# HGRN2 recurrence and multiplicative FFN: q, k and f of the first four chunks in their own buffers, issued ahead of the weights

## The chip, the cores and the metric

The kernel runs on one core of one Trainium2 chip. The metric is the device time in microseconds (us), as the median of several runs. The core has five engines with their own instruction queues: PE (TensorE, matrix products; PEld is its weight load), DVE (VectorE), ACT (ScalarE), POOL (GpSimd) and SP (SyncE). In this kernel SP issues every transfer between HBM and the on-chip memory. Each engine runs its queue strictly in the order in which the program emits it.

## What is computed

```python
def _attn_ref(q, k, v, f_logit):          # each (4, 8, 768, 48): batch, heads, steps, head size
    f = 1.0 / (1.0 + np.exp(-f_logit))
    for t in range(S):
        state = f[:, :, t, :, None] * state + np.einsum('bhd,bhe->bhde', k[:, :, t], v[:, :, t])
        y[:, :, t] = np.einsum('bhd,bhde->bhe', q[:, :, t], state)

def _moe_ref(x, w1, w2, w3, w_out):       # x (3072, 384), w1 w2 (384, 1024), w3 (1024, 1024), w_out (1024, 384)
    return ((x @ w1) * (x @ w2) @ w3) @ w_out
```

The outcome y of the recurrence, with heads side by side, is the x of the second part. The four weight matrices come as float64, so each is twice the bytes of its float32 form.

## The kernel before

**Tiling.** The 4 x 768 steps are cut into 24 chunks of 128 steps (`NU = 24`), six to a batch element. Four chunks make one FFN block of 512 rows (`NB = 6`). A chunk's work for all eight heads is laid out on 112 partitions (two groups of 48 with a gap of 16 rows) by 512 columns.

**One chunk `u`** (function `attention(u)`), with the keys of the tasks in brackets:

- loads of f, q and k (`lf`, `lq`, `lk`, L291, two DMAs of 96 KB each) and of v (`lv`, L300, one of 192 KB);
- ACT: gate = sigmoid(f) (`g`, L305). DVE: the forward product scan (`p`, L313), a reciprocal (`i`, L323), Q = q times the product (`q`, L329), the backward scan (`r`, L335), K = k times that (`k`, L343);
- PE: the K-Q pairs into PSUM (`a`, L352), ACT copies them (`m`, L361), POOL cuts them to the causal half (`c`, L367), PE multiplies by v and adds the state's share (`v`, L402 and L410 or L417);
- PE turns K (`t`, L378), ACT copies it (`e`, L386), PE forms the update of the state (`s`, L438), DVE applies it (`d`, L448 to L454), ACT lays it out for the next chunk (`b`, L460);
- ACT copies the outcome (`y`, L467). For the first four chunks PE moves it into the layout of x with the constant `perm` (`z`, L491) and ACT copies that (`x`, L496). For the others ten DMAs do it (L486).

**Buffers.** f and k have two buffers each, q three, v three, used in turn. So f of chunk 2 is loaded once the gate of chunk 0 has read its buffer, k of chunk 3 once K of chunk 1 has been formed, and so on. The gap rows 32 to 63 of every buffer are filled once by POOL in `setup()` (L235 to L237). `perm` occupies one of the four buffers of the pool "ab" until the first four chunks have been moved; POOL fills it by ten copies (L255).

**Weights.** w1 and w2 come as three pieces of 1 MB each (L879), w_out as four of 768 KB, w3 as eight of 1 MB (by the profile's list of issues). They land in five raw buffers; from the sixth piece on, a piece takes a raw buffer whose former content has been converted. Converting 512 columns to float32 takes two ACT instructions (L897, L900) and four on DVE (L903, L904, L908, L914). The FFN's first products need the first half of all three w1 pieces, the second ones that of all three w2 pieces. Later PE multiplies w3 by w_out once (L964, eight groups), so that the down product uses that single matrix; from the second block on, a scheme with seven products in place of eight is used, for which DVE forms sums.

**Order.** All tasks are entered into a planner with an engine, a cost in us, their dependencies and a priority. `Plan.order()` repeatedly takes the task that can start first by these costs, and among equals the one with the lowest priority number; the resulting order is then emitted. Transfers are two tasks: the issue on SP and the time on one modelled "DMA" engine, one after another. So a dependency in the plan only sets the place in a queue; what an instruction waits for on the chip is the data and the buffers themselves.

```python
        t["lf"] = moves(0.87, 197, 250, load(fs[u % 2], f_logit), past(u, 2, "g"), n0 - 30)
        t["lq"] = moves(0.87, 197, 250, load(qs[u % 3], q), past(u, 3, "q"), n0 - 29)
        t["lk"] = moves(0.87, 197, 250, load(ks[u % 2], k), past(u, 2, "k"), n0 - 28)
```

Here `n0` is 0, 1, 2, 3 for the first four chunks and 45 and up for the others; v has n0 - 27, the pieces of w1 have -26 to -25.8, those of w2 -16.5 to -16.3.

Of the kernel before, what the change touches and what calls it, by code (L numbers as in the profile page):

```python
# [36 lines left out]
F32 = mybir.dt.float32  # L37
# [3 lines left out]
ALU = mybir.AluOpType  # L41
AF = mybir.ActivationFunctionType
# [3 lines left out]
P = 128  # L46
# [4 lines left out]
R = 64 + D  # L51
DM = H * D
# [3 lines left out]
TB = 512  # L56
# [3 lines left out]
NQ = HP * C  # L60
# [5 lines left out]
KH = KF // 2  # L66
# [107 lines left out]
def ranged(ctx, tc, q, k, f_logit, v, w1, w2, w3, w_out, out, ident, w12, wc, left):  # L174

    nc = tc.nc
# [7 lines left out]
    abp = ctx.enter_context(tc.tile_pool(name="abp", bufs=4))  # L184
# [7 lines left out]
    gate = [keep.tile([R, NQ + 1], F32, name=f"gate{i}") for i in range(2)]  # L192
# [11 lines left out]
    def at(a, *shape):  # L204
        n = 1
        for m in shape:
            n *= m
        t = place[:, a : a + n]
        return t.rearrange("p (a b) -> p a b", a=shape[0]) if len(shape) == 2 else t
# [4 lines left out]
    wos = at(10240, KF, DM)  # L214
# [2 lines left out]
    wct = [at(6144 + KH * DH * i, KH, DH) for i in range(4)]  # L217
    ups = {(nm, i): at(a + 2 * TH * i, TH) for nm, a in (("u2", 9216), ("u3", 9216 + TH)) for i in range(2)}
    abs_ = [at(10240 + KH * P * i, KH, P) for i in range(4)]
    dns = {nm: at(12288 + DH * i, DH) for i, nm in enumerate(("m1", "u2", "u3"))}  # L220

    plan = Plan()
    plan.slot("f", NF)
    plan.slot("a", 2)
    plan.slot("ab", 4)
    moving = plan.add("PE", 0.0, lambda: None, takes=["ab"], prio=-1e9)

    def heads(t):
        return t.rearrange("p (h c) -> p h c", c=C)

    def setup():
        nc.scalar.activation(warm, nc.const_aps.tensor(0.0, (R, 1), F32), AF.Sigmoid)
        for i in range(3):
            if i < 2:
                nc.gpsimd.memset(fs[i][32:64], 30.0)  # L235
                nc.gpsimd.memset(ks[i][32:64], 0.0)
            nc.gpsimd.memset(qs[i][32:64], 0.0)  # L237
            if i == 0:
                make_identity(nc, ident)
        nc.vector.memset(floor, FLOOR)  # L240
        nc.vector.memset(heads(floor)[:, :, 0], 1.0)
        nc.vector.memset(back, 0.0)
        for t in gate:
            nc.vector.memset(t[:, NQ : NQ + 1], 0.0)
        nc.vector.memset(ones, 1.0)
        for t in sb:
            nc.vector.memset(t, 0.0)

        nc.gpsimd.memset(perm, 0.0)
        for i, (kc, hp) in enumerate(met):  # L250
            for par in range(2):
                for r, t, at_, n in runs(2 * hp + par):
                    if t == kc:
                        a = 64 * par + at_
                        nc.gpsimd.tensor_copy(perm[:, i, r : r + n], ident[0:R, a : a + n])  # L255
# [19 lines left out]
    def past(u, n, *names):  # L275
        return [tk[u - n][nm] for nm in names if u >= n and nm in tk[u - n]]

    def moves(issue, size, rate, emit, deps, prio):

        i = plan.add("SP", issue, emit, deps, prio, lag=0.6)  # L280
        return plan.add("DMA", size / rate, lambda: None, [i], prio, lag=1.3)

    def attention(u):
        s, t = st[u], tk[u]
        opens, closes = u % NCH == 0, u % NCH == NCH - 1
        n0 = need(u)

        def load(dst, src):
            def emit():
                for par in range(2):  # L290
                    nc.sync.dma_start(dst[rows(par)], src[u, par])  # L291
            return emit

        t["lf"] = moves(0.87, 197, 250, load(fs[u % 2], f_logit), past(u, 2, "g"), n0 - 30)
        t["lq"] = moves(0.87, 197, 250, load(qs[u % 3], q), past(u, 3, "q"), n0 - 29)
        t["lk"] = moves(0.87, 197, 250, load(ks[u % 2], k), past(u, 2, "k"), n0 - 28)

        def load_v():
            s["v"] = loads.tile([P, DM], F32, name="vt")
# [2 lines left out]
        t["lv"] = moves(0.45, 197, 320, load_v, past(u, 3, "v", "s"), n0 - 27)  # L302

        def gates():
            nc.scalar.activation(gate[u % 2][:, 0:NQ], fs[u % 2][0:R], AF.Sigmoid)  # L305

        t["g"] = plan.add("ACT", 0.65, gates, [t["lf"]] + past(u, 2, "r") + past(u, 3, "d"), n0)
        if not opens:
# [17 lines left out]

        def scale_q():
            s["Q"] = work3.tile([R, NQ], F32, name="Q")
            nc.vector.tensor_tensor(s["Q"], qs[u % 3][0:R], s["P"], ALU.mult)  # L329

        t["q"] = plan.add("DVE", 0.7, scale_q, [t["p"], t["lq"]] + past(u, 3, "v", "a"), n0 + 0.1)

# [7 lines left out]

        def scale_k():
            s["K"] = work.tile([R, NQ], F32, name="K")
            nc.vector.tensor_tensor(s["K"], ks[u % 2][0:R], s["R"], ALU.mult)  # L343

        t["k"] = plan.add("DVE", 0.7, scale_k, [t["r"], t["lk"]] + past(u, 2, "a", "t"), n0)

        def pairs():
            s["pa"] = ps.tile([P, 2, NQ], F32, name="pa")
# [498 lines left out]
            q["m4"]["frees"].append(first_ab[1])  # L847


    pieces, folds, users = {}, [], []  # L850
    parts, w12_sums, wc_sums, joins, spot = [], [], [], {}, [0]

    def fetch(loads_, a, prio, subs, deps=()):

        total = subs[-1][1]
        if not wide:  # L860
            def plain():
                for place_, src in loads_:
                    for c0, c1, dst, _, _ in subs:
                        d = dst().rearrange("p (a m) -> p a m", a=a)
                        m = (c1 - c0) // a
                        b0 = c0 // a if len(subs) > 1 else 0
                        nc.sync.dma_start(d[place_], src[:, :, b0 : b0 + m])
            waits = [d for sub in subs for d in sub[4]]
            ld = plan.add("SP", 1.9 * total / 512, plain, waits, prio, lag=2.0)
            return [ld] * len(subs)  # L870
        load_no = len(users)
        buf = load_no if load_no < len(raws) else (load_no - len(raws)) % NRAW
        raw = raws[buf][:, 0 : 2 * total]
        words = raw.rearrange("p (n two) -> p n two", two=2)
        held = [g for no, b_, gs in users if b_ == buf for g in gs]

        def load():
            for place_, src in loads_:
                nc.sync.dma_start(raw.rearrange("p (a m) -> p a m", a=a)[place_], src.bitcast(U32))  # L879

        ld = moves(0.45, total, 380, load, held[-2:], prio)
        got = []
        users.append((load_no, buf, got))
        ends = []

        def sub(c0, c1, dst, due, waits):
            n = c1 - c0
            w = n / 512
            lo, hi = words[:, c0:c1, 0], words[:, c0:c1, 1]
            a0 = spot[0] if n <= 512 else (spot[0] + 512) // 1024 * 1024 % 2048  # L890
            spot[0] = (a0 + (512 if n <= 512 else 1024)) % 2048
            m = magnitudes[:, a0 : a0 + n]
            mine = range(a0 // 512, (a0 + n + 511) // 512)
            s = {}

            def magnitude():
                nc.scalar.activation(m, hi.bitcast(F32), AF.Abs)  # L897

            def rest():
                nc.scalar.activation(lo.bitcast(F32), lo, AF.Copy, bias=2.0, scale=2.0**-51)  # L900

            def shifted():
                nc.vector.tensor_scalar(m, m, HIGH, LOW, ALU.min, ALU.max)  # L903
                nc.vector.tensor_scalar(m.bitcast(U32), m.bitcast(U32), 3, None, ALU.logical_shift_left)  # L904

            def signed():
                s["to"] = dst()
                nc.vector.scalar_tensor_tensor(  # L908
                    s["to"].bitcast(U32), hi, 0x80000000, lo, ALU.bitwise_and, ALU.bitwise_or
                )  # L910

            def joined():
                to = s["to"].bitcast(I32)
                nc.vector.tensor_tensor(to, m.bitcast(I32), to, ALU.add)  # L914

            past = [joins[i] for i in mine if i in joins]
            b = plan.add("ACT", 0.2 + 0.43 * w, magnitude, [ld] + past, due)
            e = plan.add("ACT", 0.2 + 0.43 * w, rest, [ld], due)
            h = plan.add("DVE", 0.32 + 0.54 * w, shifted, [b], due)
            g = plan.add("DVE", 0.16 + 0.53 * w, signed, [e, b] + list(waits), due)  # L920
            j = plan.add("DVE", 0.16 + 0.53 * w, joined, [h, g], due - 1)
            parts.append((g, j))
            joins.update({i: j for i in mine})
            got.append(g)
            ends.append(j)

        for one_ in subs:
            sub(*one_)
        return ends

    def weights():
# [16 lines left out]
        def held(buf):  # L948
            return [g for _, b, gs in users if b == buf for g in gs]

        done = []
        for i in range(0, KF, 2):
            src = w_out[i * P : (i + 2) * P].rearrange("(kc p) c -> p kc c", p=P)
            done += fetch([(slice(0, P), src)], 2, 25 + 2.2 * i, [(
                0, 2 * DM, lambda i=i: wos[:, i : i + 2].rearrange("p a c -> p (a c)"), 45 + 2.2 * i, held(4),
            )])

        w3s = {}
# [71 lines left out]
        nc.vector.tensor_scalar(left, count, R - 0.5, None, ALU.is_lt)  # L1030

    setup()
    weights()
    for u in range(NU):
        attention(u)
        if u == NU - 1:
            judged = plan.add("DVE", 1.5, judge, [tk[i]["y"] for i in range(NU)], -20)
        if u % UB == UB - 1:
            ffn(u // UB)
# [340 lines left out]
```

## Time and profile before

| | |
|---|---|
| median of 4 runs | 509.95 us (508.39 to 511.66) |
| the profiled execution: its own time | 512.46 us |
| its span, first to last instruction | 510.6 us |
| PE busy | 489.1 us (96%) |
| DVE busy | 362.3 us (71%) |
| ACT busy | 162.3 us (32%) |
| POOL busy | 41.1 us (8%) |
| first matmul starts | 8.42 us |
| first FFN product starts (L512) | 41.88 us |
| mean granted PE clock | 0.993 |

The share of busy time is an average over stages. The page's second part cuts the span into 40 slices of 12.8 us with a digit for each engine: 9 is 90% busy or more. The chain of waits follows the work that ended last backwards through what released it. In its lines the first number is the start in us, the second the length; "SPq" is SP issuing a transfer, "DMA k" the time until that transfer landed.

### The profile page before, as it was taken

The numbers are of one execution on the slowest core, as the hardware profiler recorded it, in microseconds if no ns is written. First come the engines' busy times: TensorE is split into PE (matmuls) and PEld (weight loads), VectorE is DVE, ScalarE is ACT, GpSimd is POOL, SyncE is SP. The second block draws the span as 40 slices with busy tenths as digits, with TensorE's granted clock in tenths as the row PEclk, the third lists the DMA queues.
The fourth block names the chain that finished last, engine by engine and source line by source line (L and its number), as shares of the span: only waits on it lengthen the run. The fifth ranks groups of instructions, "written<-read, shape, count | busy, mean of one in ns | idle before, by whom it ended". The sixth has DMA issues, their size and how long they took to land.

```text
span 510.6 us, 8802 instructions
## 1 busy us (share of the span) xinstructions
PE 489.1 (96%) x3346; PEld 409.4 (80%) x3346; DVE 362.3 (71%) x701; ACT 162.3 (32%) x340; POOL 41.1 (8%) x48
## 2 busy tenths in 40 slices
PE   3879999999999999999999999999999999999995
PEld 2769754666689877889888889888899888889994
DVE  6869899999998749965678666255564677665541
ACT  3759545754334426311342112321010011011000
POOL 7120010110102111000210000010000000000000
PEclk9979999999999999999999999999999999999999
DMA  5986455854222356311251001210002100000011
GB/s 166 376 234 203 142 190 215 284 186 120 77 62 76 86 147 197 98 38 28 59 168 44 1 3 31 59 51 0 2 21 58 48 1 0 1 0 1 31 50 50
DMA packets 30163, 46.02 MB, mean 90 GB/s; under 512 B 6560, under 2 KB 20384, under 8 KB 28320
## 3 DMA queue, kind: packets, MB, share of 16 engines
q1 hardware_dynamic: 30112, 45.38, 28.8%
q8 instruction: 28, 0.46, 0.4%
q14 instruction: 23, 0.19, 0.1%
HBM read 36.70 MB, written 4.72 MB: 81 GB/s over the span
## 4 chain that ended last, share of the span: by engine, by line
PE 89%; DMA 5%; DVE 2%; SPq 1%; issue 1%; POOL 0%; ACT 0%; DVEq 0%; POOLq 0%; ACTq 0%
PE f L512 66%; PE f L964 8%; PE pa L352 4%; PE pa L402 4%; DMA k<-in_k_dram 2%; DMA vt<-in_v_dram 2%; PE pk L438 2%; PE pa L417 2%; PE pk L378 2%; DMA q<-in_q_dram 1%; SPq L291 1%; PE f L410 1%; PE f L402 1%; PE f L491 1%; DMA f<-in_f_logit_dram 0%
## 5 line engine op out<-in xcount | busy, mean ns | idle before, releaser
L512 PE MATMUL f<-xt,w 128*128 128x256 f32 (+1 forms) x600 | 159.6, 397 | 0.0
L512 PEld LDWEIGHTS f<-xt,w 128*128 128x128 f32 x600 | 113.0, 190 | 24.5 <-issue 10.0
L512 PE MATMUL f<-place 128*128 128x192 f32 (+1 forms) x504 | 114.1, 351 | 0.0
L512 PEld LDWEIGHTS f<-place 128*128 128x128 f32 x504 | 87.3, 190 | 6.9 <-issue 1.1
L367 POOL TENSOR_SCALAR_AFFINE_SELECT A<-A 128x1024 f32<-128x1024 f32 x24 | 31.6, 1316 | 299.8 <-ACT A L361 299.8
L964 PE MATMUL f<-place 128*128 128x384 f32 x128 | 43.1, 490 | 0.0
L615 ACT COPY a<-f 128x256 f32<-128x256 f32 x36 | 13.4, 372 | 78.0 <-PE f L512 59.5
L512 PE MATMUL f<-xt,place 128*128 128x256 f32 x144 | 37.1, 380 | 0.0
L964 PEld LDWEIGHTS f<-place 128*128 128x128 f32 x128 | 23.8, 190 | 15.8 <-issue 0.5
L512 PE MATMUL f<-wc,ab 128*128 128x192 f32 x192 | 35.6, 329 | 0.0
L352 PEld LDWEIGHTS pa<-Q,K 48*128 48x128 f32 x384 | 25.8, 204 | 10.4 <-issue 8.1
L352 PE MATMUL pa<-Q,K 48*128 48x128 f32 x384 | 30.5, 303 | 3.3 <-DVE K L343 3.3
L512 PEld LDWEIGHTS f<-wc,ab 128*128 128x128 f32 x192 | 31.8, 190 | 0.9
L313 DVE TENSOR_TENSOR_SCAN fwd<-gate,floor 112x512 f32<-112x512 f32 x24 | 30.2, 1257 | 2.7 <-ACT gate L305 1.9
L361 ACT COPY A<-pa 128x1024 f32<-128x1024 f32 x24 | 24.2, 1010 | 24.0 <-PE pa L352 24.0
L639 DVE TENSOR_TENSOR place<-f,a 128x256 f32<-128x256 f32 x36 | 15.3, 424 | 23.3 <-PE f L512 23.2
L335 DVE TENSOR_TENSOR_SCAN bwd<-gate,back 112x512 f32<-112x512 f32 x24 | 29.7, 1238 | 0.8
L512 PEld LDWEIGHTS f<-xt,place 128*128 128x128 f32 x144 | 26.9, 189 | 3.6 <-DVE place L639 0.2
L343 DVE TENSOR_TENSOR K<-k,bwd 112x512 f32<-112x512 f32 x24 | 17.6, 733 | 9.3 <-DMA k<-in_k_dram 5.9
L897 ACT ACTIVATE place<-place 128x512 f32<-128x512 f32 (+2 forms) x24 | 21.2, 885 | 8.7 <-DVE w L914 4.5
L467 ACT ACTIVATE ys<-pa 112x512 f32<-112x512 f32 x20 | 11.9, 596 | 36.4 <-PE pa L417 21.1
L900 ACT ACTIVATE place<-place 128x512 f32<-128x512 uint32 (+2 forms) x24 | 21.1, 892 | 7.4 <-DMA place<-in_w_out_dram 4.2
(97 smaller groups left out, 620.5 us busy)
## 6 DMA issues: line engine op xcount, KB each, us to landing
place<-in_w_dram SPq DMA_DIRECT2D x14, 1024.0 KB, 5.4
f<-in_f_logit_dram SPq DMA_DIRECT2D x48, 96.0 KB, 2.7
q<-in_q_dram SPq DMA_DIRECT2D x48, 96.0 KB, 2.7
k<-in_k_dram SPq DMA_DIRECT2D x48, 96.0 KB, 2.5
vt<-in_v_dram SPq DMA_DIRECT2D x24, 192.0 KB, 3.1
out_dram<-o SPq DMA_DIRECT2D x24, 192.0 KB, 2.0
place<-in_w_out_dram SPq DMA_DIRECT2D x4, 768.0 KB, 5.3
xt<-ys SPq DMA_DIRECT2D x120, 24.0 KB, 1.8
```

What stands on the lines that cost most here:

```text
L313: nc.vector.tensor_tensor_scan(s["P"], gate[u % 2][:, 0:NQ], floor, 0.0, ALU.mult, ALU.max)
L335: nc.vector.tensor_tensor_scan(s["R"][:, ::-1], gate[u % 2][:, NQ:0:-1], back[:, ::-1], 0.0, ALU.mult, ALU.max)
L343: nc.vector.tensor_tensor(s["K"], ks[u % 2][0:R], s["R"], ALU.mult)
L352: nc.tensor.matmul(s["pa"][:, par, cols], lhsT=s["K"][rows(par), cols], rhs=s["Q"][rows(par), cols], start=True, stop=True,)
L361: nc.scalar.copy(s["A"].rearrange("p r h c -> p r (h c)"), s["pa"])
L367: nc.gpsimd.affine_select(out=a, in_=a, pattern=[[0, H], [1, C]], compare_op=ALU.is_ge, fill=0.0, base=0, channel_multiplier=-1,)
L402: nc.tensor.matmul(y_block(b)[64 * half : 64 * half + w], lhsT=s["v"][:, h * D : h * D + w], rhs=s["A"][:, par, hp], start=bank not in met ...
L512: nc.tensor.matmul(out_, lhsT=lhs[i], rhs=rhs[i], start=start and i == 0, stop=i == len(lhs) - 1, skip_group_check=True,)
L639: nc.vector.tensor_tensor(ups["u3", k], q["Y"], q["a"], ALU.add)
L897: nc.scalar.activation(m, hi.bitcast(F32), AF.Abs)
L900: nc.scalar.activation(lo.bitcast(F32), lo, AF.Copy, bias=2.0, scale=2.0**-51)
L964: nc.tensor.matmul(w3s["p", jc], lhsT=w3s[jc][:, kc * P : kc * P + P], rhs=wos[:, kc], start=(kc == 0), stop=(kc == KF - 1),)
```

## The change

- k of chunks 2 and 3 and f of chunks 2 and 3 get a place of their own: one more of the four "ab" buffers, called `early`, held until K of chunks 2 and 3 has been formed (the task `coming`). q of chunk 3 gets a place inside the tile `place`, which w_out takes later; the conversion of w_out waits for Q of chunk 3.
- For the first four chunks the loads of f, k and q have no dependency. Their priorities are n0 - 30, n0 - 29.5 and n0 - 29, in that order (before: f, q, k with -30, -29, -28). All weight tasks are entered after the fourth chunk's.
- From chunk 4 on the buffers go round as before (f and k two, q three), and the plan lets these loads start only after the fifth weight piece (`asked[4]`, the second of w2) has landed.
- `setup()` fills the gap rows of the new places: two memsets of 32 x 1024 and one of 32 x 512 more on POOL, ahead of `perm`.

```diff
+    early = abp.tile([P, KH, TB], F32, name="ab")[0:R]
+    ks += [early[:, 0], early[:, 1]]
+    fs += [early[:, 2], early[:, 3]]
+    qs.append(at(12288, NQ)[0:R])
...
+    coming = plan.add("PE", 0.0, lambda: None, takes=["ab"], prio=-1e9)
...
+        nc.gpsimd.memset(early[32:64, 2:4], 30.0)
+        nc.gpsimd.memset(early[32:64, 0:2], 0.0)
+        nc.gpsimd.memset(qs[2][32:64], 0.0)
+        nc.gpsimd.memset(qs[3][32:64], 0.0)
...
-        t["lf"] = moves(0.87, 197, 250, load(fs[u % 2], f_logit), past(u, 2, "g"), n0 - 30)
-        t["lq"] = moves(0.87, 197, 250, load(qs[u % 3], q), past(u, 3, "q"), n0 - 29)
-        t["lk"] = moves(0.87, 197, 250, load(ks[u % 2], k), past(u, 2, "k"), n0 - 28)
+        fu, qu, ku = (x[u if u < 4 else u % n] for x, n in ((fs, 2), (qs, 3), (ks, 2)))
+
+        def free(n, *names):
+
+            if u < 4:
+                return []
+            return asked[4:5] + [tk[u - n if u - n >= 4 else u % n][nm] for nm in names]
+
+        t["lf"] = moves(0.87, 197, 250, load(fu, f_logit), free(2, "g"), n0 - 30)
+        t["lk"] = moves(0.87, 197, 250, load(ku, k), free(2, "k"), n0 - 29.5)
+        t["lq"] = moves(0.87, 197, 250, load(qu, q), free(3, "q"), n0 - 29)
...
+        if u in (2, 3):
+            t["k"]["frees"].append(coming)
...
         ld = moves(0.45, total, 380, load, held[-2:], prio)
+        asked.append(ld)
...
-                0, 2 * DM, lambda i=i: wos[:, i : i + 2].rearrange("p a c -> p (a c)"), 45 + 2.2 * i, held(4),
+                0, 2 * DM, lambda i=i: wos[:, i : i + 2].rearrange("p a c -> p (a c)"), 45 + 2.2 * i,
+                held(4) + [tk[3]["q"]],
...
     setup()
-    weights()
     for u in range(NU):
         attention(u)
+        if u == 3:
+            weights()
```

More of the change, by code (lines that the diff above doesn't have):

```diff
@@ L232, in setup @@
         nc.scalar.activation(warm, nc.const_aps.tensor(0.0, (R, 1), F32), AF.Sigmoid)
[L233 to L236, printed above, removed]
+        for i in range(2):
+            nc.gpsimd.memset(fs[i][32:64], 30.0)
+            nc.gpsimd.memset(ks[i][32:64], 0.0)
             nc.gpsimd.memset(qs[i][32:64], 0.0)
@@ L304, in gates @@
         def gates():
-            nc.scalar.activation(gate[u % 2][:, 0:NQ], fs[u % 2][0:R], AF.Sigmoid)
+            nc.scalar.activation(gate[u % 2][:, 0:NQ], fu, AF.Sigmoid)
         t["g"] = plan.add("ACT", 0.65, gates, [t["lf"]] + past(u, 2, "r") + past(u, 3, "d"), n0)
@@ L328, in scale_q @@
             s["Q"] = work3.tile([R, NQ], F32, name="Q")
-            nc.vector.tensor_tensor(s["Q"], qs[u % 3][0:R], s["P"], ALU.mult)
+            nc.vector.tensor_tensor(s["Q"], qu, s["P"], ALU.mult)
         t["q"] = plan.add("DVE", 0.7, scale_q, [t["p"], t["lq"]] + past(u, 3, "v", "a"), n0 + 0.1)
@@ L342, in scale_k @@
             s["K"] = work.tile([R, NQ], F32, name="K")
-            nc.vector.tensor_tensor(s["K"], ks[u % 2][0:R], s["R"], ALU.mult)
+            nc.vector.tensor_tensor(s["K"], ku, s["R"], ALU.mult)
         t["k"] = plan.add("DVE", 0.7, scale_k, [t["r"], t["lk"]] + past(u, 2, "a", "t"), n0)
+        if u in (2, 3):
+            t["k"]["frees"].append(coming)
         def pairs():
@@ L847, in ffn @@
             q["m4"]["frees"].append(first_ab[1])
-    pieces, folds, users = {}, [], []
+    pieces, folds, users, asked = {}, [], [], []
     parts, w12_sums, wc_sums, joins, spot = [], [], [], {}, [0]
```

## The prediction

> **What bounds the kernel now.** I read the page's slices first, for where PE is not busy.
>
> ```profile
> PE   3879999999999999999999999999999999999995
> DVE  6869899999998749965678666255564677665541
> PEclk9979999999999999999999999999999999999999
> ```
>
> PE is full from the fourth slice (38 us) to the last. The open part is the first 38 us: PE starts at 8.42 us, and the third slice is at 7 in both busy share and clock. The busy table by stretch gives that hole its size (the columns PE, PEld, DVE, ACT, POOL are busy us, then clock, DMA share, GB/s):
>
> ```profile
> 24.00:26.95 2.95, 2.95 (x42) 2.53 (x40) 2.74 (x5) 2.95 (x7) 0.71 (x1) 1.00 1.05 361
> 26.95:30.23 3.28, 0.01 (x1) 0.03 (x1) 0.83 (x2) 0.76 (x2) 0.77 (x1) 0.82 0.99 321
> 30.23:36.10 5.87, 5.87 (x42) 5.31 (x43) 5.70 (x12) 2.28 (x4) 1.36 (x1) 0.52 0.71 177
> 42.04:87.24 45.20, 45.20 (x212) 30.15 (x212) 42.51 (x74) 27.78 (x48) 1.42 (x1) 1.00 0.57 183
> 87.24:141.40 54.16, 54.16 (x335) 33.69 (x335) 52.77 (x68) 29.18 (x46) 5.16 (x4) 1.00 0.54 174
> 141.40:384.00 242.60, 241.36 (x1895) 209.65 (x1894) 166.71 (x344) 69.50 (x165) 19.85 (x15) 1.00 0.22 62
> ```
>
> PE stands still for 3.28 us and then runs 5.87 us at clock 0.52. From 42 to 384 us it is idle for 1.24 us in all. DVE is 94% and 97% busy from 42 to 141 us. The chain of waits names the cause of the hole:
>
> ```profile
> 10.83 7.14 DMA vt<-in_v_dram
> 17.98 0.02 issue
> 17.99 0.33 SPq L879
> ...
> 18.42 0.37 SPq L291
> 18.79 0.04 issue
> 18.84 10.46 DMA k<-in_k_dram
> ...
> 29.39 0.70 DVE K L343
> 30.10 0.14 issue
> 30.23 2.08 PE pa L352 x16
> 32.31 1.90 PE f L402 x15
> 34.21 1.90 PE f L410 x8
> 36.11 0.38 PE pk L378 x4
> 36.49 1.02 PE f L402 x15
> ```
>
> k of chunk 3 is issued at 18.42 us, behind three or four 1 MB weight pieces, and lands at 29.3, 10.46 us later (k's median over the run is 2.5 us). It was issued that late for two reasons. It needs the buffer of k of chunk 1. And SP has at most eight DMAs under way: the weight piece at 17.99 starts the moment v of chunk 1 has landed, which is the eighth DMA before it. The last lines show the clock's price: the same 15 matmuls of L402 take 1.90 us cold and 1.02 us warm.
>
> **The change, part by part.**
>
> *Issue order on SP.* A 96 KB load costs SP 0.44 us (0.87 for two), a v load 0.42. By the priorities the first 26 DMAs are 24 q, k and f loads with v of chunks 0 and 1 among them, then w1's three pieces, v of chunk 2, two w2 pieces. Before, 19 DMAs took from 1.35 to 10.36 us, 0.47 each; so w1 starts at 1.35 + 26 x 0.47 = 13.6 instead of 10.36. The other two w1 pieces went out at 13.54 and 13.97 before and go at about 14.0 and 14.5 now. All f, k, q of the first four chunks are out by 13.5 and down by 16, k of chunk 3 at about 13 instead of 29.3. The limit of eight does not bite: eight issues take 3.5 us, landing takes 2.3 to 2.8.
>
> A rule speaks against this order: the Trainium skill, "DMA: Bandwidth & Descriptors", section "Bandwidth", says to batch transfers to 1 MiB or more for three quarters of peak. The row behind it here: in the first 8 us of the run DMA share was 0.49 at 142 GB/s, with small loads only, against 0.99 to 1.05 later. By the rule the weights should lead: 3.2 us of half-used engines is lost to w1. By the trace that is covered. ACT first waited for w1 until 17.37 us (1.5 us), and DVE's first conversion ran only at 25.29. With w1's first piece landing at 13.6 + 4.4 (the shortest landing of a piece) = 18.0 and each next one about 3.5 us later (f of chunk 4, held by the eight, was let go by the second piece at 21.6, v of chunk 3 by the third at 24.9: 3.4 apart), all w1 is in by 25. Without that cover the price is the 3.2 us. I take 0.
>
> *POOL.* The memset of 32 x 512 takes 0.52 us; the two of 32 x 1024 are bounded by twice that, so 2.6 us more ahead of the ten copies that ended at 10.41, now 13.0. Behind them is the first causal cut, which started at 12.54 (its input at 12.47): 0.4 us later. Its product at 15.23 waits on PE behind L378, which waits for DVE's K; so 0. SP waits for these memsets too: that of f for chunk 2 ends by about 5.4, its load is issued at 6.9. 0.
>
> *v of chunk 0* moves from 6.17 to about 8.9 and lands at 11.3 to 12.1 (2.4 to 3.2 us). L438 used it at 11.34. So 0 to 0.7 us on chunk 1, since DVE's S stands ahead of K there; I take 0.4. v of chunk 3 waits for chunk 0's last use (17.2) and lies behind two w2 pieces, at about 31; before, it was first used 4.2 warm us of PE after K of chunk 3. So the covering work just ends there.
>
> *DVE.* Two waits for k go: 1.22 us (chunk 2) and 2.62 us (chunk 3), and 1.5 us of conversion that stood before the second are done after it. The first may come back: S of chunk 1 stands behind K of chunk 2 and waits for PE until 19.7. So K of chunk 3 starts at 29.39 - 2.62 - 1.48 + 0.4 = 25.7, or 24.5 if the 1.22 is kept.
>
> *PE.* At 25.7 + 0.8 = 26.5 its pairs are ready; PE's earlier work ended at 26.95 (plus up to 0.4). So the gap closes. From 30.23 to 42.04 PE was busy without a break, 11.81 us; L352, L402 and L410 cold took 2.08 + 1.90 + 1.90 against 1.09 + 1.02 + 1.06 warm, 2.7 us more. Warm it is 9.1, and FFN starts at 27.2 + 9.1 = 36.3 instead of 42.04: 5.7 us earlier. Its first weights: three conversions at 2.15 us and the state's 0.9 us after K give 25.7 + 0.7 + 7.4 + 0.8 (a stretched one, as L904's 1.20 us) = 34.6. In time.
>
> The clock is where a rule and the trace differ. Here a gap of 3.28 us cost 5.87 us at half clock, 2.7 us. The skill's page "TensorE: Matmul & The Clock Gate" gives one idle window of about 3.4 us for going cold and as much busy time for getting warm: by that no loss, or 1.7 us. The trace decides: 2.7. If a gap of 1 to 2 us stays, the page says warm; the trace shows no such gap, so its price lies between 0 and 2.7. I take 0, since the gap closes.
>
> *Downstream.* The gain has to pass the stage in which DVE is 94 to 97% busy. DVE itself is ahead by 29.39 - 25.7 = 3.7 (its 1.5 us of moved work included: 2.2), plus the 1.54 us it waited for ACT at 37.98 (ACT waited for the cold L410): 3.7 net. The slacks add: conversion of the last w2 piece ended about 1.2 us before PE needed it at 54.81, that of the last w_out piece at 84.91 for the fold at 87.24, 2.3 us. So PE can keep 3.7 + 1.2 = 4.9 of its 5.7. Loads from chunk 4 on are asked for after w2; they were first used at 43.99. 0.
>
> Sum: 0 (start) - 5.7 (hole and clock) + 0.8 (DVE) = -4.9. Against the profiled execution (span 510.6, its own time 512.46) that is a span of 505.7 and a time of 507.6. The median of the runs, 509.95, gives 505.0.
>
> **The rivals.**
>
> *The gain stays in the start.* Chunk 1 a full 0.7 us late, the S wait back, a gap that keeps the clock cold for 2.7 us, w1 landing late: 5.7 - 0.3 - 2.7 - 1 = 1.7, so 508.3. For it: ACT waits in order for w1, DVE is the fuller engine after 42 us. Against: PE has 9 us of queued work there.
>
> *SP's queue blocks the late weights (slower).* SP is in order. k of chunk 6 was issued at 68.05, when K of chunk 4 had been formed, and v at 76.95 after chunk 4's products; the last w_out piece went at 62.2, ahead of both. The plan is drawn anew, and if it puts that piece behind such a v, it goes 14.7 us later; less the slack of 2.3 and the 4.9 won, 7.5 us are lost: 517.4. Behind the k alone (5.9 us) nothing is lost on balance. It decides from about 10 us of delay. Against: the plan's costs put it right before, and chunk 4's work keeps its late priority.
>
> *It doesn't do what it says:* k of chunk 3 still late, by the limit of eight or by a memset. The issue times above exclude both; 510.
>
> *More:* the 1.22 us and all of DVE's stalls kept: 6.5 us, 503.5.
>
> **The numbers.** -4.9 (503.9 to 507): 0.50. More than 6: 0.09. Stays in the start: 0.17, of which a third is still faster by over 0.5% (2.55 us, about what a measurement of this kernel can tell from no change). SP blocks or another re-drawn queue: 0.22, nearly all slower. Nothing: 0.02. So faster 0.63, same 0.15, slower 0.22. The range runs from 502.5 to 514: it leaves out half of the slower cases and a little below.
>
> **What would show it.** K of chunk 3 on DVE before 26.5 us without a DMA wait; no PE gap over 1 us after 20 us and clock 1.00 from there; first L512 at 35.5 to 37.5; first w1 piece down at 17.5 to 18.5; first fold (L964) at 82 to 83.5; no new idle time on PE after that. It is wrong if L512 starts on time but the fold does not, if ACT or DVE waits for w1 by more than 3 us, or if SP waits for a K or a product with w_out or w3 behind it.

## The result, and the profile after

| | before | after |
|---|---|---|
| median, all runs | 509.93 us (63 runs, 507.43 to 514.33) | 508.46 us (42 runs, 506.56 to 511.26) |
| ratio after / before | | 0.9969, 95% interval 0.9959 to 0.9980 |
| the profiled execution's own time | 512.46 us | 506.82 us |
| its span | 510.6 us | 504.5 us |
| first FFN product, first fold (w3 by w_out; L964, now L984), on PE's timeline | 41.88, 87.24 us | 36.28, 83.10 us |

The change makes the kernel 0.31% faster, about 1.5 us, where 4.9 us were forecast. The two profiled executions differ by 5.6 us in their own times. So the profiles seem to say that the forecast came true, and the medians say that two thirds of it did not. Both profiles are out of the ordinary: the one before lies 2.5 us above its kernel's median, the one after 1.6 us below, the second shortest of the 44 executions of the changed kernel that have a recorded clock. Most of what follows is about that contradiction.

The page's slices after the change (tenths busy, 12.6 us each; line numbers after the change are 8 to 20 higher than before):

```profile
PE   3899999999999999999999999999999999999995
PEclk9999999999999999999999999999999999999999
```

The 7 of the third slice is gone from PE and from the clock. The busy table by stretch, with the columns as before:

```profile
24.00:26.95 2.95, 2.79 (x34) 2.48 (x32) 2.88 (x5) 2.95 (x6) 1.02 (x1) 1.00 1.02 429
26.95:30.23 3.28, 3.28 (x52) 2.77 (x50) 3.21 (x5) 3.17 (x7) 1.67 (x2) 1.00 0.86 351
30.23:36.10 5.87, 4.67 (x56) 3.99 (x56) 5.66 (x14) 3.99 (x10) 0.04 (x1) 1.00 0.68 203
36.28:83.10 46.82, 46.82 (x227) 31.68 (x225) 45.04 (x78) 29.92 (x54) 1.42 (x1) 1.00 0.59 190
```

The stretch 26.95 to 30.23, in which PE stood still before, is full; the next runs at clock 1.00, with 1.2 us of new waiting in it. After 36.28 us nothing new is lost: the last row has PE busy throughout, so has the stretch from there to 135.5, and in the 244.5 us after that PE is idle for 0.70. The span is 6.1 us shorter, though the fold starts only 4.1 us earlier. The other 2.0 us lie behind the fold; half of them are waits of PE for K (0.7 us) and for v (0.3) that the profile before has there and this one has not. The chain of waits shows what holds the start now:

```profile
13.45 6.91 DMA place<-in_w_dram
20.39 1.59 DVE Q L345
...
25.41 0.68 DVE Q L345
...
32.25 0.43 DVE place L923
33.08 0.61 PE pk L396 x4
...
36.35 1.49 PE f L530 x6
```

k is no longer in it. From 20.4 to 32.7 us the chain runs through DVE: Q and K of the chunks, then three weight conversions. PE's own timeline has the new wait (start, length, what ran, and in brackets the idle time before it and its cause):

```profile
26.44 1.16 PE L370 MATMUL pa<-Q,K 48*128 48x128 f32 x16
...
33.08 0.61 PE L396 MATMUL pk<-ident,K 112*128 112x112 f32 x4 [1.01 <-DVE S L471]
...
36.28 1.56 PE L530 MATMUL f<-xt,w 128*128 128x256 f32 x6
...
39.03 2.32 PE L530 MATMUL f<-xt,w 128*128 128x256 f32 x10
```

The pairs of chunk 3 (L370) start at 26.44 without a wait. PE then waits 1.01 us for S, the state after chunk 2 (L471), which stands behind those conversions on DVE.

### The profile page after: what moved, and what is told of

Its sections match the earlier page's. It is cut to its first block, busy times and chain, and to the rows that moved or that the text cites. A ratio compares the mean times of both kernels' runs of the same rounds, so it can differ in the third digit from the quotient of the medians.

```text
span 504.5 us, 8806 instructions
## 1 busy us (share of the span) xinstructions
PE 486.2 (96%) x3346; PEld 407.2 (81%) x3346; DVE 362.4 (72%) x701; ACT 162.6 (32%) x340; POOL 42.5 (8%) x51
## 4 chain that ended last, share of the span: by engine, by line
PE 92%; DVE 2%; DMA 1%; POOL 1%; SPq 1%; issue 1%; POOLq 0%; DVEq 0%
PE f L530 69%; PE f L984 8%; PE pa L370 4%; PE pa L420 4%; PE pa L435 2%; PE pk L456 2%; PE pk L396 2%; DMA place<-in_w_dram 1%; SPq L299 1%; DVE Q L345 0%; DVE w L933 0%; DVE w L927 0%; PE f L509 0%; DVE bwd L351 0%; DVE fwd L329 0%
## 5 line engine op out<-in xcount | busy, mean ns | idle before, releaser
L984 PE MATMUL f<-place 128*128 128x384 f32 x128 | 43.1, 490 | 0.0
L984 PEld LDWEIGHTS f<-place 128*128 128x128 f32 x128 | 23.8, 190 | 15.8 <-issue 0.5
L370 PEld LDWEIGHTS pa<-Q,K 48*128 48x128 f32 x384 | 24.8, 198 | 6.9 <-issue 4.2
L370 PE MATMUL pa<-Q,K 48*128 48x128 f32 x384 | 29.5, 296 | 0.0
L485 ACT ACTIVATE ys<-pa 112x512 f32<-112x512 f32 x20 | 11.9, 598 | 40.6 <-PE pa L435 23.0
L396 PE MATMUL pk<-ident,K 112*128 112x112 f32 x80 | 12.3, 280 | 11.2 <-DVE K L359 10.2
```

What stands on the lines that cost most here:

```text
L370: nc.tensor.matmul(s["pa"][:, par, cols], lhsT=s["K"][rows(par), cols], rhs=s["Q"][rows(par), cols], start=True, stop=True,)
L396: nc.tensor.transpose(out=s["pk"][:, hp], in_=s["K"][:, hp * C : hp * C + C], identity=ident[0:R, 0:R])
L984: nc.tensor.matmul(w3s["p", jc], lhsT=w3s[jc][:, kc * P : kc * P + P], rhs=wos[:, kc], start=(kc == 0), stop=(kc == KF - 1),)
```

## The experiments

Kernels tried together shared their runs of the kernel before; each ratio below is against those. For every execution there is its time, span and mean granted clock, and the experiments use both the medians and these lists. Kernels with extra matmuls compute with them nothing that is used. Each kernel's line numbers are its own.

**The kernel before, profiled again (e1).** No edit.

> The kernel before, unchanged, for the span and clock of many executions and for a second profile. Theory A (the 3.3 us gap of PE costs the cold clock, 2.7 us, in every execution): spans near 510 us with a mean clock of about 0.993 and little spread, and the second profile shows clock near 0.5 after the gap again. Theory B (the cold clock is paid only in some executions, and the profile shown was one of them): spans mostly 507 to 509 with a mean clock of 0.997 to 0.999, some near 510.5 with 0.993; a second profile more likely shows clock 1.00 after the gap.

Measured: ratio 1.0007 [0.9989, 1.0025], so nothing new in the times. But the profile is another one. PE's timeline in the first profile of the kernel before, then in this one (an execution like the first is called early-warm below, one like the second late-warm):

```profile
17.13 1.96 PE L352 MATMUL pa<-Q,K 48*128 48x128 f32 x16
...
19.62 1.60 PE L491 MATMUL f<-ys,ab 112*128 112x128 f32 x12
```

```profile
17.12 2.08 PE L352 MATMUL pa<-Q,K 48*128 48x128 f32 x16
...
20.15 2.93 PE L491 MATMUL f<-ys,ab 112*128 112x128 f32 x12
...
29.64 1.16 PE L352 MATMUL pa<-Q,K 48*128 48x128 f32 x16 [0.84 <-DVE K L343]
...
84.05 5.32 PE L964 MATMUL f<-place 128*128 128x384 f32 x16
```

Up to 17.12 us the two agree to 0.01 us. Then PE gets its full clock at about 19 us in the one and only at about 23 in the other (12 matmuls of L491 in 1.60 us, or in 2.93). In the late case PE reaches chunk 3 so much later that it waits 0.84 us for K instead of 3.28, its clock does not fall, and the fold starts at 84.05 instead of 87.24.

The clocks of all executions say how often each happens. Over all comparisons the unchanged kernel has 208 executions with a recorded clock:

| mean clock | executions | median time |
|---|---|---|
| 0.995 or less | 93 (45%) | 511.20 us |
| 0.997 or more | 113 (54%) | 508.95 us |
| between | 2 | |
| the changed kernel: 0.997 or more in all | 44 | 508.46 us |

The profile on which the prediction rests (clock 0.993) is of the first kind.

The lists show two more things. The median span fell from 508.1 to 506.2 us, 1.9 us and not 1.5: an execution takes 1.8 to 2.0 us more than its span in the kernel before and 2.1 to 2.6 in the changed one, so 0.4 us of the gain is lost outside the span. Why is not shown. And of the changed kernel's 44 spans, 40 lie between 505.3 and 507.2; the profiled one, 504.5, stands almost alone. How many of the 44 warmed early is not on record.

**The kernel before, profiled twice more (e12, e16).** No edit.

> One more profile of the unchanged kernel before. If the gap and its half clock come from how early PE warms up: either full speed by 19 us, a gap of about 3 us at 27 to 30 us and clock 0.991 to 0.995, or full speed at 23 us, a gap under 1.5 us and clock 0.997 or more. A late warm-up with a cold gap, or an early one without, would speak against it.

> A further profile of the unchanged kernel before: either full speed by about 19 us, gap of 2.4 us or more, half clock, clock 0.991 to 0.995, first fold at 87 us; or full speed at about 23 us, gap under 1.5 us, clock 0.997 or more, first fold at 84 us.

Measured: spans 511.8 and 509.8, clocks 0.992 and 0.990. The busy table and PE's timeline of e12:

```profile
30.23:36.10 5.87, 5.87 (x43) 5.23 (x40) 5.47 (x10) 2.65 (x5) 1.35 (x1) 0.50 0.73 194
```

```profile
19.85 1.60 PE L491 MATMUL f<-ys,ab 112*128 112x128 f32 x12
...
29.66 2.08 PE L352 MATMUL pa<-Q,K 48*128 48x128 f32 x16 [2.48 <-DVE K L343]
...
87.12 3.07 PE L964 MATMUL f<-place 128*128 128x384 f32 x9
```

e16 gives the same: the 12 matmuls of L491 in 1.60 us at 19.50, a wait of 2.96 us for K up to 29.94, L352 in 2.08 us, the fold from 86.91.

So in four profiles of the kernel before, the three with a low mean clock all warmed early, waited 2.5 to 3.3 us for K of chunk 3, ran on at half clock and folded at 86.9 to 87.2; the one with a high clock did none of it and folded at 84.05.

**The hole filled in the kernel before (e2).** 24 matmuls of no use ahead of chunk 3's pairs, so that PE does not stand still while k is late.

```diff
+            for _ in range(24 if u == 3 else 0):
+                nc.tensor.matmul(s["pa"][:, 0, 0:C], lhsT=ident, rhs=ident, start=True, stop=True)
```

> Before, with 24 extra 128x128 matmuls at the head of the pairs of chunk 3 (3.3 us of PE work that waits for nothing), so that the gap is filled and the clock stays up, while K of chunk 3 is as late as before. Theory A: 2.5 us faster than before (ratio 0.995). Theory B: 0 to 1 us faster (0.998 to 1.000). If the extra matmuls overrun the gap: up to 1 us slower.

Measured: 512.09 us, ratio 1.0041 [1.0021, 1.0062], slower. As a measure of what the cold clock costs it failed, since it was made too large:

```profile
29.44 5.62 PE L350 MATMUL pa<-ident 128*128 128x128 f32 x48
```

The 24 took 5.62 us (0.234 each; the trace has two records for each), and in this late-warm execution (12 matmuls of L493 in 2.93 us) there was hardly a hole to fill: the first FFN product started at 44.00. What it does show is in the clocks: 0.997 or more in all 13 executions, where the kernel before had 17 of 45 at 0.995 or less. The low clock comes from the wait for k.

**Which part of the change does it: k alone (e3, e4).** k of chunks 2 and 3 in a place of their own, f and q as before. In e3 with the old priorities, in e4 also asked for ahead of the weights:

```diff
+    ks += [early[:, 0], early[:, 1]]
...
-        t["lk"] = moves(0.87, 197, 250, load(ks[u % 2], k), past(u, 2, "k"), n0 - 28)
+        t["lk"] = moves(0.87, 197, 250, load(ku, k), past(u, 2, "k") if u >= 4 else [], n0 - 28)                         # e3
+        t["lk"] = moves(0.87, 197, 250, load(ku, k), past(u, 2, "k") if u >= 4 else [], n0 - (29.5 if u < 4 else 28))    # e4
```

> Only k of chunks 2 and 3 in a place of their own; priorities and everything else as before. If the shared buffer is what makes k of chunk 3 late, it lands by 17 us, K of chunk 3 runs near 24.5 and the kernel gains what the change gains (0.997). If its place in SP's queue behind the weights and the limit of eight transfers under way do it, k is still issued near 18 us and lands near 29, and the time is as before (1.000).

> As the one before, and k of the first four chunks asked for ahead of the weights (priority n0 - 29.5); f and q keep their shared buffers and the weights their place among the tasks. If k of chunk 3 was the whole hole, K of chunk 3 runs at 23 to 25 us, PE has no gap and the kernel gains as much as the full change (0.997) or a little more, since the conversion of the weights and S of chunk 2 stand in another order. If f and q matter as well: about 0.9985.

Measured: e3 508.40 us, ratio 0.9989 [0.9971, 1.0008]; e4 507.98 us, ratio 0.9962 [0.9946, 0.9978]. PE's timeline of e3, then of e4:

```profile
28.38 1.16 PE L359 MATMUL pa<-Q,K 48*128 48x128 f32 x16 [1.46 <-DVE K L348]
```

```profile
27.57 1.16 PE L359 MATMUL pa<-Q,K 48*128 48x128 f32 x16 [0.82 <-DVE Q L334]
...
84.40 5.32 PE L971 MATMUL f<-place 128*128 128x384 f32 x16
```

A buffer of its own does not settle it. In e3 k of chunk 3 is still issued at 18.28 us and takes over 7 us to land; the wait shrinks to 1.46 us, and 4 of 12 executions still have a clock of 0.995 or less. The ratio's interval holds no gain, and nearly the full one. With the early request as well, none of 17 has, and the gain is that of the full change. So k needs the early place in SP's queue as well as the buffer; the two intervals overlap, and it is the clocks that tell them apart. f and q of chunks 2 and 3 in places of their own add nothing that these intervals can tell. The profile of e3 is early-warm (12 matmuls of L498 at 19.45 us take 1.60 us) and keeps its clock; its fold starts at 83.88. The profile of e4 is of a late-warm execution (12 matmuls of L498 at 19.11 us take 2.93 us), and its fold (84.40) is no earlier than e1's: where PE is late anyway, an early k brings nothing in these two traces. The 17 spans of e4 fall into two groups, 7 at 503.8 to 505.2 us and 10 at 506.0 to 507.7; the full change has only 3 of 44 below 505.3. Why, and whether the first group are the early-warm ones, is not known.

**The changed kernel again (e5).** No edit.

> The changed kernel, unchanged, for a second profile. In the first one PE's matmuls had full speed from 19.0 us; in the second profile of the kernel before only from 22.9 us (the twelve L491 matmuls took 2.93 us there, 1.60 in the first). If it is by chance when PE warms up, this profile may show either, and if late, a span near 506 us instead of 504.5, with K of chunk 3 at 25 to 26.5.

Measured: 508.88 us, span 506.6. PE's timeline:

```profile
20.31 2.93 PE L509 MATMUL f<-ys,ab 112*128 112x128 f32 x12
...
83.99 5.32 PE L984 MATMUL f<-place 128*128 128x384 f32 x16
```

A late-warm execution of the changed kernel. Its fold at 83.99 stands against 84.05 for the late-warm one of the kernel before, and 83.10 against 87.1 for the early-warm ones (mean of 87.24, 87.12 and 86.91). By these traces the change takes 4.0 us out of the one kind up to the fold and 0.1 out of the other; the spans of the two late-warm ones are 506.3 us before and 506.6 after.

**PE warmed from the start: a first attempt (e6, e7).** 11 matmuls of no use at the very start and 6 more before chunk 1's transposes, on the changed kernel (e6) and on k alone early (e7).

```diff
+        for _ in range(11):
+            nc.tensor.matmul(hot[:, 0, 0:C], lhsT=ident, rhs=ident, start=True, stop=True)
...
+                for _ in range(6 if u == 1 else 0):
+                    nc.tensor.matmul(s["pk"][0:R, 0], lhsT=ident[0:R, 0:R], rhs=ident[0:R, 0:R], start=True, stop=True)
```

> The changed kernel with 11 extra 128x128 matmuls from about 3 us on and 6 extra of 112x112 ahead of chunk 1's L396, so that PE is at full speed by 8.4 us and stays so. Extra work of no use to the output. If the doubled durations until 19 or 23 us sit on the path to the first FFN product (S of chunk 1 waits 1.2 to 1.6 us for PE, then Q of chunk 2): 1.5 to 2.5 us faster than the changed kernel (ratio to before 0.992 to 0.994) and a smaller spread. If the start is bound by DVE and the transfers, not by PE: as the changed kernel (0.997). If the extra matmuls run over: up to 1 us slower than it.

> The kernel with only k of the first four chunks early, with the same extra matmuls. As above: 1.5 to 2.5 us faster than without them (0.991 to 0.993) if the cold start is on the path, else 0.996.

Measured: e6 509.06 us, 0.9980 [0.9961, 0.9998]; e7 508.25 us, 0.9974 [0.9958, 0.9989]; neither ratio below that of the kernel it was built on, so the 0.991 to 0.994 of the expectations did not come. In e6 PE's clock had fallen again at 11.9 us, before the second batch, which then took 2.58 us and pushed chunk 1's transposes to 16.23 us (14.3 in the kernel before).

**DVE's order in the changed kernel (e8).** The wait of 1.01 us for S of chunk 2 suggests putting S ahead of the second conversion.

```diff
-            h = plan.add("DVE", 0.32 + 0.54 * w, shifted, [b], due)
+            h = plan.add("DVE", 0.32 + 0.54 * w, shifted, [b] + list(waits) * (n == 512), due)
...
-                        due[which, half] + 0.1 * kc, [],
+                        due[which, half] + 0.1 * kc, [tk[2]["d"]] if (which, kc, half) != (0, 0, 0) else [],
```

> The changed kernel with S of chunk 2 put ahead of the second weight conversion in DVE's queue (one more dependency in the plan). In the profile PE waited 1.01 us for it at 33.08 us. If that wait is part of what is missing of the forecast: up to 1 us faster than the changed kernel (0.995). If the conversion then becomes what the first FFN product waits for: the same (0.997) or slower by 0.5 us.

Measured: 510.35 us, ratio 1.0007 [0.9984, 1.0029]: the gain is lost. The profile is of a late-warm execution (L509 in 2.93 us, as in e5). DVE's timeline has

```profile
32.66 0.36 DVE L471 TENSOR_TENSOR S<-pk,S 112x192 f32<-112x192 f32 x1 [4.00 <-PE pk L456]
```

DVE now stands idle for 4.00 us until PE has formed the update, the conversions behind it are late, and the second group of the fold waits 2.3 us for one by the list of PE's waits. That wait is new: e5, late-warm as well, has none before its fold. The planner's order, S behind three conversions, was the better one.

**Both kernels with PE warm from 8 us on (e9, e10, e11).** This removes the chance of the two kinds of start: 11 matmuls of no use at the start, 4 before the state update of chunk 0 (L438), 7 before the transposes of chunk 1 (L378), on the kernel before (e9), the changed one (e10), and k alone early (e11).

```diff
+    def keep_hot(n):
+        for _ in range(n):
+            nc.tensor.matmul(hot[0][:, 0:C], lhsT=ident, rhs=ident, start=True, stop=True)
```

> The kernel before with PE kept busy from 3 us on: 11 extra 128x128 matmuls ahead of the first L378, 4 ahead of chunk 0's L438, 7 ahead of chunk 1's L378 (22 of no use to the output, into a spare PSUM bank). Theory 1 (in most executions PE is at half speed until 23 us, and it is this, not k of chunk 3, that sets the start): with PE at full speed by 8.4 us PE stands before k of chunk 3 again, a gap of 3 us or more and then half clock, as in the first profile of before: spans as the slower group of before or 0.5 us under it, no gain on the median (1.000). Theory 2 (the slow start of PE is hidden beside DVE): as before in all respects (1.000), gap 0.8 us.

> The changed kernel with the same 22 extra matmuls. Theory 1: with the k wait gone and PE warm, K of chunk 3 runs by 24 us and the first FFN product by 36: 2 to 3 us faster than the changed kernel (ratio 0.991 to 0.993), so that the change is worth 4 us or more between the two warm kernels. Theory 2: no gain, 0.997.

> Only k of the first four chunks early, with the same 22 extra matmuls. Theory 1: as the one before, 0.990 to 0.993. Theory 2: 0.996.

Measured, with 22 executions each: e9 511.07 us, 1.0016 [0.9999, 1.0034]; e10 508.81 us, 0.9971 [0.9950, 0.9992]; e11 508.81 us, 0.9971 [0.9954, 0.9987]. PE's timeline of e9, then of e10:

```profile
30.16 2.08 PE L360 MATMUL pa<-Q,K 48*128 48x128 f32 x16 [3.94 <-DVE K L351]
...
87.29 3.07 PE L976 MATMUL f<-place 128*128 128x384 f32 x9
```

```profile
24.99 1.60 PE L521 MATMUL f<-ys,ab 112*128 112x128 f32 x12 [1.48 <-ACT ys L497]
26.53 2.05 PE L378 MATMUL pa<-Q,K 48*128 48x128 f32 x16
```

The kernel before, warmed early by force, gives the picture of its slower kind: a wait of 3.94 us, half clock, fold at 87.29. Its clock is at 0.995 or less in 16 of 22 executions. Against it the change gains 0.9971 / 1.0016 = 0.9955, some 2.3 us in place of 1.5 (a quotient of two ratios; its interval was not measured). That is short of the 4 us expected between the two warm kernels, and of the 0.990 to 0.993 expected of e10 and e11. One reason shows in the trace: the warmed changed kernel has a new wait of 1.48 us, for ACT's copy, and falls to half clock behind it (L378 takes 2.05 us); 14 of the 22 executions of e10 and 12 of e11 are at 0.995 or less.

**The hole filled as well (e13, e14, e15).** 14 more matmuls of no use at chunk 3's pairs in e9, 10 there in e11, 6 before the move of chunk 1's outcome (L509, L521 in e10) in e10:

```diff
+            for _ in range(14 if u == 3 else 0):                                     # e13; 10 in e15
+                nc.tensor.matmul(s["pa"][:, 0, 0:C], lhsT=ident, rhs=ident, start=True, stop=True)
...
+            for _ in range(6 if u == 1 else 0):                                      # e14
+                nc.tensor.matmul(s["px"][:, 0], lhsT=ident, rhs=ident, start=True, stop=True)
```

> The warm kernel before (22 extra matmuls early), with 14 more extra matmuls (3.3 us) at the head of chunk 3's pairs, so that PE is busy while it would wait for k of chunk 3; k itself is as late as before. If the half clock after the gap is what the slow group pays: clock 0.997 or more in nearly all executions, first FFN product at 39.3 us instead of 41.9, ratio to before 0.996 to 0.998 instead of 1.0016. If it is the late k alone: first FFN product stays at 41.9 and the ratio at 1.001.

> The warm changed kernel with 6 more extra matmuls (1.4 us) ahead of chunk 1's L521, where PE stood for 1.48 us and went to half clock for 4 us. If that half clock holds it back: 1 to 2 us faster than without them (ratio to before 0.993 to 0.995). If DVE's conversions set the first FFN product (it started at 36.7 us with and without warm-up): the same, 0.997.

> The warm kernel with only k early, with 10 more extra matmuls (2.3 us) ahead of chunk 3's pairs, where PE waited 2.48 us for Q. If half clock holds it back: 0.993 to 0.995; if DVE does: 0.997.

Measured: e13 510.02 us, 1.0010 [0.9995, 1.0025]; e14 507.60 us, 0.9949 [0.9934, 0.9964]; e15 507.22 us, 0.9952 [0.9932, 0.9971]. PE's timeline of e13, then of e14:

```profile
28.94 1.16 PE L362 MATMUL pa<-Q,K 48*128 48x128 f32 x16 [0.18 <-DVE K L351]
...
83.72 5.32 PE L978 MATMUL f<-place 128*128 128x384 f32 x16
```

```profile
81.92 5.32 PE L998 MATMUL f<-place 128*128 128x384 f32 x16
```

In the profiled execution of e13 k is as late as ever (pairs at 28.94, against 26.43 in e14), but PE stays warm, and the fold comes at 83.72. That is 3.6 us ahead of e9 (87.29), the same kernel with the hole open, and 1.8 us behind e14 (81.92), the changed kernel with PE kept warm as well. So in these three traces the half clock costs twice as much as the lateness of k itself. The executions agree on the second part: the 13 of e13 with a clock of 0.997 or more have a median of 508.85 us, against 507.60 for e14, 1.25 us (part of that may be work, since e13 has 8 more useless matmuls, 1.9 us at e2's 0.234 each).

The profiled execution of e13 is the second fastest of its 22. In its median e13 gained nothing, where 0.996 to 0.998 was expected: 6 of the 22 still had a clock of 0.995 or less (median 510.97), and a fixed number of matmuls does not fit every execution. e14 has 0.997 or more in all 21, and its fold is the earliest of all. It and e15 are the fastest kernels here, some 0.5% ahead of the kernel before. Their advantage over the change itself was only seen through two comparisons (0.9949 [0.9934, 0.9964] and 0.9969 [0.9959, 0.9980]); these intervals overlap a little.

## Why the prediction was right in the profile and wrong in the median

**Right: the mechanism.** k of chunk 3 was late because of its place in SP's queue, PE stood still for it and ran at half clock behind. The change takes all of that away, by k's place (e4). "It doesn't do what it says" is out.

**Right: most steps of the sum, for an execution of the kind that was profiled.** The first w1 piece was issued at 13.45 (13.6 was worked out), the pairs of chunk 3 found K formed, the clock was full (one gap of 1.01 us stayed, where none over 1 us was to), the fold at 83.10 lay in the range given. Against the profiled execution's own time 507.6 was forecast, and 506.82 came. That closeness is partly luck: up to the fold 4.1 us were won where 4.9 were forecast, and the 2.0 us behind the fold were not foreseen.

**Wrong, and decisive: "The median of the runs, 509.95, gives 505.0".** The prediction saw that its profile's own time, 512.46, was 2.5 us above the median, and still subtracted from the median the whole of a hole that only that profile showed. The 2.5 us were the hole, or most of it: 45% of the executions have a low clock and a median of 511.20, the others 508.95, 2.25 us less. Weighed so, removing the half clock is worth 0.45 x 2.25 = 1.0 us, an estimate. The remaining 0.5 us is the distance from 508.95 to the changed kernel's 508.46; late-warm profiles of both kernels fold at the same time (84.05, 83.99), so this part has no mechanism shown. A term that the prediction left out altogether is the 0.4 us more outside the span: it went from a span of 505.7 to a time of 507.6 with the distance of the kernel before, 1.9 us, where the changed kernel has 2.3.

**Wrong in size: the gap of 3.28 us as a gain.** The prediction counted 3.28 us of idle time and 2.7 us of half clock as one hole, 5.7 us, cut to 4.9 by DVE. PE's first FFN product at 36.28 is where it was forecast, but by luck: six of its matmuls only passed the move of chunk 3's outcome, and the rest begin at 39.03, as if all had begun at 37.6. Against 41.88 that is 4.2 us in place of 5.7, and the fold won 4.1 us, not 4.9. Most of what is missing is 1.2 us of new waiting between 30.23 and 36.10 us. Behind the gap stands DVE: in the changed kernel it is 97% busy from 24.00 to 36.10 us with Q, K and the conversions that the FFN needs, and S of chunk 2 goes through it late. e9, e13 and e14 separate the two terms where PE is kept warm: 3.6 us at the fold for the half clock, 1.8 for the late k.

**Wrong without consequence.** The first w1 piece landed at about 20.3 (ACT waited 0.52 us for it), not at 17.5 to 18.5; DVE had no time for a conversion before 26.01 us anyway. The rule that the prediction took from the Trainium skill, "DMA: Bandwidth & Descriptors", section "Bandwidth", speaks of the size of transfers and not of their order; the 3.2 us that the prediction drew from it as a price for later weights were not lost here. The parts of its chances for a faster kernel add up to 0.65, not to the 0.63 given. The wait for k on chunk 2 came back as a wait of DVE for PE, 1.19 us before S of chunk 1, as the prediction allowed.

**The clock's price.** The prediction set the trace's 2.7 us against the 0 or 1.7 us that it drew from the Trainium skill's "TensorE: Matmul & The Clock Gate" and chose the trace. That was right for the profiled kind: the clock column in quarters of a microsecond shows half clock for 6.8 us there. That page's section "Part 1: The HAM clock gate" also says that the window runs freely and that the length of a cold start differs between runs of one kernel. That sentence spoke against reading one profile as all of them, and it was not weighed. Here the start's half clock ended at about 19 or at about 23 us.

**The rivals.** The measured time, 508.46, lies on the price of "the gain stays in the start" (508.3), but by other steps: of that rival's only the wait for S came back (1.19 us). No gap stayed that cools the clock, v of chunk 0 held PE up by 0.21 us, and w1 held ACT up by 0.52. The slower rival, SP's queue holding the late weights, is excluded by the busy table, with 0.7 us of PE idle in all from 36.28 to 380 us.

## What to carry to other kernels

Before a hole in a profile is subtracted from a median, ask whether every execution has it: if the profiled execution's own time or its clock stands off the others by about the size of the hole, count the executions on each side and weigh the gain by their share. Ask the same of the profile after, which lay 1.6 us below its median here. A short wait of PE may cost more through the clock that it takes away than through its own length (in this kernel the half clock cost about twice what the late k did), so shorten first the waits that are followed by half clock in the profile. Filling them with useless matmuls helps only where the number fits every execution: in e14 the clock stayed up in all 21, in e13 it fell in 6 of 22. And a change that takes away the last wait of an engine pays only up to the next engine's chain, so add up that engine's work to the next meeting point before counting the gap as won.

## What the runs showed of the hardware that was not expected

- **An earlier full clock made the kernel before slower.** The three profiled executions whose PE warmed at about 19 us folded at 86.9 to 87.2 us, the one at about 23 us folded at 84.05: an earlier PE waited longer for k (2.5 to 3.3 us against 0.84), lost its clock, and paid more than it had won. What decides between 19 and 23 us is open; up to 17.12 us the first profile and e1 agree.
- **The half clock comes in pieces of 3.4 us.** Read in quarters of a microsecond, the clock column shows it from 29.1 to 35.9 us in the first profile, 29.4 to 36.3 in e12, 28.7 to 35.5 in e16, 29.25 to 36.1 in e9 and 11.9 to 18.7 in e6 and e7, 6.8 us each time; but from 26.6 to 30.0 in e10 and 25.5 to 28.9 in e11, 3.4 us. The first and last quarters of the first profile, then of e10:

```profile
29.00:29.25 0.25, 0.00 (x0) 0.00 (x0) 0.00 (x0) 0.00 (x0) 0.00 (x0) 0.65 0.99 369
...
35.75:36.00 0.25, 0.25 (x4) 0.25 (x3) 0.25 (x1) 0.00 (x0) 0.00 (x0) 0.70 0.82 150
```

```profile
26.50:26.75 0.25, 0.25 (x3) 0.23 (x4) 0.25 (x1) 0.25 (x1) 0.25 (x1) 0.69 0.70 295
...
29.75:30.00 0.25, 0.25 (x6) 0.25 (x4) 0.25 (x2) 0.25 (x1) 0.24 (x1) 0.50 0.46 156
```

In the two short ones PE was at work from the fall on. In the long ones it still waited in the first 3.4 us: for 0.2 to 1.3 us in the first four, for 1.19 us in e6 and 0.92 in e7. This fits the freely running window of about 3.4 us of the Trainium skill's "TensorE: Matmul & The Clock Gate", "Part 1: The HAM clock gate", with two windows in place of the one that the prediction took.
- **A wait shorter than that window was enough.** Waits of 2.48, 2.96 and 3.28 us before K led to half clock. Near 1.5 us it went both ways: 1.46 us (e3) did not, 1.42 us for v (e6) and 1.48 us (e10) did. So length alone does not decide there.
- **The clock column does not count the cold start.** In the first 17 us of the kernel before matmuls take nearly twice their later time (L378: 0.98 and 0.55 us) while the column says 1.00. So its mean compares later stretches only.
